# Sink-window attention into a balanced mixture of experts: a new plan of the experts' work, and gathered rows transposed in halves of 64

## The chip, the cores and the metric

One core of one Trainium2 chip runs the whole program as one launch. The metric is device time in microseconds (us), from three timed runs of the kernel before: 525.15, 525.58 and 529.23, median 525.58. All times inside the kernel come from one further execution that was profiled; it took 527.85 us, of which 526.1 us are the span from the first instruction to the last.

## The reference

Attention with 4 batches, 8 heads, 768 positions and head size 64, in which a position sees the first 4 keys and its own 128 last ones; then its rows (3072 x 512) go through a mixture of 8 experts in which every expert gets exactly 384 rows, handed out greedily from the largest logit down:

```python
scores = scale * np.matmul(q, k.transpose(0, 1, 3, 2))
keep = is_sink | in_window
...
a = a / (np.sum(a, axis=-1, keepdims=True) + 1e-09)
x = np.matmul(a, v)            # rows: 3072 x 512
...
logits = x @ w_gate            # 3072 x 8
for idx in np.argsort(-logits.flatten()):
    tok, e = idx // E, idx % E
    if assigned[tok] >= 0 or counts[e] >= 384: continue
    assigned[tok] = e; counts[e] += 1
...
out[mask] = np.maximum(x[mask] @ w1[e], 0.0) @ w2[e]   # 512 -> 1024 -> 512, per expert
```

## The kernel before, in words

The first 155 us of the span are the attention, in 24 blocks of 128 rows. It writes its rows to DRAM (`x_dram`). The change does not touch it. It does hold one thing that matters here: its transposes at L101 and L113 work on 64 rows at a time, the upper and the lower 64 rows of the array side by side, and write to two banks of PSUM.

Then come the experts, one after the other in an order that the router finds out. Router `k` (class `R`, method `phase`) finds the expert that fills up next and its 384 rows. It is a chain of six steps. In each, VectorE compares (`cmp`, L488), TensorE counts (L558, "cnt", 12 or 6 small products), VectorE turns the counts into a decision (`i`, L580), TensorE spreads it (L584, "dp", one small product), and VectorE prepares the next compare. After the sixth step come the ranks (L605, "pp") and the lookup of the row numbers (L631, "ip", 12 small products), from which VectorE writes `idx`.

With `idx`, GpSimd gathers the 384 rows from `x_dram` by three indirect DMAs (L674, G) into `xg0` to `xg2`, 128 rows each. TensorE transposes them (L682, X): 4 column chunks of 128 times 3 row tiles make 12 transposes of 128x128 for each expert, into `pt0` and `pt1`, one PSUM bank for a chunk (for expert 0 also `py0` and `py1`). ScalarE writes the rounded high part `xh` of each chunk (L684), VectorE the remainder `xl` (L685).

SyncE loads an expert's weights in 8 pieces (L665) through 4 buffers `raw`. ScalarE makes the high part `wh` (L667), VectorE the low part `wl` (L669). The first layer (M, L695) has 8x4 steps of three products (`M k.f.c`, for 128 columns `f` of the hidden layer and chunk `c`); its result is split into `hh` on ScalarE (L698) and `hl` on VectorE (L699). The second layer (N, L707) has 3x8 steps `N k.t.f` of three products; ScalarE copies its result to `yo` (L710), and GpSimd scatters it to the output (L712, S). Scatters wait for the one before them to land, and gathers and scatters share GpSimd's queue.

All eight experts, with their routers, are one graph of some 1,800 work pieces (`Graph.add`): an engine, a length in ns, what a piece reads and writes. `ML` holds a delay for each pair of engines (E TensorE, A ScalarE, V VectorE, P GpSimd, S SyncE, D the DMA queue). `Graph.order` is a list planner: it steps through planned time, and on each engine takes, among the pieces that can start within a window (`WIN`) of the earliest, the one of the highest priority: its longest path to the end plus a number for its class (`BIAS`). The order that comes out is the order in each engine's queue. An engine never leaves it: an instruction that waits holds up all behind it. Where the plan shows TensorE idle before the first expert's products, `run` puts filler products there (L534).

Of the kernel before, what the change touches and what calls it, by code (L numbers as in the profile page):

```python
# [377 lines left out]
CAP=384  # L378

STEPS=[(26,64),(20,64),(15,32),(10,32),(5,32),(0,32)]  # L380
ML={'VV':127,'EV':200,'EA':220,'VE':215,'AE':205,'AV':142,'VA':130,'AP':180,'PV':180,'PE':215,'VP':180,'PA':180,'PP':60,'AA':35,'EE':0,
    'VS':900,'SD':1100,'VD':1250,'PD':1250,'AD':1250,'ED':1250,'DA':900,'DV':900,'DP':900,'DE':1070,'DD':0,'EP':220,'PQ':1560,}

class Graph:
# [18 lines left out]
    def order(self,bias,win,free):  # L403
# [37 lines left out]
class Moe:  # L441
# [80 lines left out]
    def pools(self,ctx,w1,w2,x_dram,out):  # L522
# [7 lines left out]
        self.pt=ring(2,[128,512],F32,"pt",ps); self.ph=ring(2,[128,512],F32,"ph",ps); self.py=ring(2,[128,512],F32,"py",ps); self.pr=ring(2,[128,512],F32,"pr",ps)  # L530
# [140 lines left out]
    def rows(self,g,k):  # L671
        nc=self.nc; idx=self.idx[k]; b=k%2
        for t in range(3):
            g.add('P',1038,lambda t=t: nc.gpsimd.indirect_dma_start(out=self.xg[t],out_offset=None,in_=self.x_dram,in_offset=bass.IndirectOffsetOnAxis(ap=idx[:,t:t+1],axis=0)),  # L674
                  [f'idx{k}'],[f'xgi{t}',f'xg{t}'],f'G{k}.{t}',f'G{k}')
            g.add('D',728,None,[f'xgi{t}'],[f'xg{t}'],f'g{k}.{t}',f'G{k}',lat=2300)
        for c in range(4):

            tp,tn=(self.py[c%2],f'py{c%2}') if k==0 and c>1 else (self.pt[c%2],f'pt{c%2}')
            pts=[tn,tn+'.1',tn+'.2']  # L680
            for t in range(3):
                g.add('E',110,lambda t=t,c=c,tp=tp: nc.tensor.transpose(tp[:,128*t:128*t+128],self.xg[t][:,128*c:128*c+128],self.idn),  # L682
                      [f'xg{t}'],[pts[t]],f'X{k}.{c}.{t}',f'X{k}')
            g.add('A',371,lambda c=c,tp=tp: nc.scalar.activation(self.xh[b][:,c,:],tp[:,0:CAP],AF.Copy),pts,[f'xh{b}.{c}'],f'xh{k}.{c}',f'X{k}')  # L684
            g.add('V',469,lambda c=c,tp=tp: nc.vector.tensor_tensor(self.xl[b][:,c,:],tp[:,0:CAP],self.xh[b][:,c,:].bitcast(F32),OP.subtract),pts+[f'xh{b}.{c}'],[f'xl{b}.{c}'],f'xl{k}.{c}',f'X{k}')  # L685

    def mlp(self,g,k):
        nc=self.nc; b=k%2; cls=f'M{k}'; idx=self.idx[k]
        for f in range(8):
            s=(8*k+f//2)%self.NW; p=self.ph[f%2]; pn=f'ph{f%2}'  # L690
            wh,wl=[a[s].rearrange("p (d f) -> p d f",d=4)[:,:,128*(f%2):128*(f%2)+128] for a in (self.wh,self.wl)]
            for c in range(4):
                def mm(c=c,p=p,wh=wh,wl=wl):
                    for i,(x,y) in enumerate(((wh,self.xh[b]),(wh,self.xl[b]),(wl,self.xh[b]))):
                        nc.tensor.matmul(p[:,0:CAP],x[:,c,:],y[:,c,:],start=c==0 and i==0,stop=c==3 and i==2)  # L695
# [141 lines left out]
```

## Time and profile before

| | us |
|---|---|
| median of three runs (525.15 to 529.23) | 525.58 |
| profiled execution | 527.85 |
| its span | 526.1 |
| attention, to the first router product | 155.5 |
| router 0, up to the first row transposes | 155.5 to 184.8 |
| eight experts on TensorE | 184.8 to 519.4 |
| last copy and scatter | to 526.1 |

Busy shares of the span are 91% for TensorE, 72% for VectorE, 44% for ScalarE and 29% for GpSimd. In the experts TensorE is the engine to watch: an idle time of another engine costs nothing unless TensorE waits for it.

### The profile page before, as it was taken

The numbers are of one execution on the slowest core, as the hardware profiler recorded it, in microseconds if no ns is written. First come the engines' busy times: TensorE is split into PE (matmuls) and PEld (weight loads), VectorE is DVE, ScalarE is ACT, GpSimd is POOL, SyncE is SP. The second block draws the span as 40 slices with busy tenths as digits, with TensorE's granted clock in tenths as the row PEclk, the third lists the DMA queues.
The fourth block names the chain that finished last, engine by engine and source line by source line (L and its number), as shares of the span: only waits on it lengthen the run. The fifth ranks groups of instructions, "written<-read, shape, count | busy, mean of one in ns | idle before, by whom it ended". The sixth has DMA issues, their size and how long they took to land. (4 is left out here: it accounts for less than half of the span.)

```text
span 526.1 us, 11023 instructions
## 1 busy us (share of the span) xinstructions
PE 480.9 (91%) x3958; PEld 398.8 (76%) x3958; DVE 378.4 (72%) x1188; ACT 232.4 (44%) x666; POOL 150.3 (29%) x195
## 2 busy tenths in 40 slices
PE   5999999999974779989998998999999989999994
PEld 3788786877862359868877976878878868999983
DVE  3999999999986776876796896897788765542100
ACT  4877887777710342243154262263054254441110
POOL 3886775574410200040033030031041031200011
PEclk8999999999995597997999999999999999999998
DMA  7757666754320640380093272290183395610011
GB/s 224 251 144 208 178 179 171 210 172 127 98 61 1 210 172 1 128 292 20 10 317 116 63 256 83 88 330 25 60 260 121 119 281 199 206 56 21 21 39 41
DMA packets 75319, 73.11 MB, mean 139 GB/s; under 512 B 28544, under 2 KB 57856, under 8 KB 75264
## 3 DMA queue, kind: packets, MB, share of 16 engines
q1 hardware_dynamic: 71424, 59.81, 37.4%
q0 software_dynamic: 3840, 12.59, 6.8%
q8 instruction: 31, 0.51, 0.4%
q14 instruction: 24, 0.20, 0.1%
HBM read 59.80 MB, written 12.58 MB: 138 GB/s over the span
## 5 line engine op out<-in xcount | busy, mean ns | idle before, releaser
L667 ACT ACTIVATE wh<-raw 128x1024 fp32r<-128x1024 f32 x64 | 67.8, 1060 | 102.0 <-DMA raw<-w 61.8
L669 DVE TENSOR_TENSOR wl<-raw,wh 128x1024 fp32r<-128x1024 f32 x64 | 77.9, 1220 | 34.9 <-ACT wh L667 31.7
L695 PE MATMUL ph<-xh,wh 128*128 128x384 f32 x256 | 93.6, 366 | 2.4 <-DVE hl L699 2.4
L695 PE MATMUL ph<-xh,wl 128*128 128x384 f32 x256 | 87.8, 343 | 0.0
L695 PE MATMUL ph<-xl,wh 128*128 128x384 f32 x256 | 87.8, 343 | 0.0
L707 PE MATMUL py<-wh,hh 128*128 128x512 f32 x192 | 78.8, 411 | 0.2 <-ACT yo L710 0.2
L712 POOL DMA_INDIRECT out<-yo,idx x24 | 27.9, 1164 | 177.9 <-ACT yo L710 119.5
L698 ACT ACTIVATE hh<-ph 128x384 fp32r<-128x384 f32 x64 | 30.9, 488 | 107.1 <-PE ph L695 77.4
L707 PE MATMUL py<-wh,hl 128*128 128x512 f32 x192 | 75.7, 394 | 0.1
L707 PE MATMUL py<-wl,hh 128*128 128x512 f32 x192 | 75.6, 394 | 0.0
L95 ACT ACTIVATE P<-pp,nmx 128x132 f32<-128x132 f32 x192 | 68.6, 371 | 8.6 <-DVE nmx L90 8.1
L674 POOL DMA_INDIRECT xg<-x_dram,idx x24 | 29.3, 1221 | 136.1 <-PE py L707 70.5
L80 PE MATMUL pp<-kk,q 64*128 64x260 f32 (+1 forms) x384 | 58.5, 405 | 7.3 <-POOL q L73 3.8
L699 DVE SCALAR_TENSOR_TENSOR hl<-ph,hh 128x384 fp32r<-128x384 f32 x64 | 35.2, 554 | 36.0 <-ACT hh L698 35.4
L695 PEld LDWEIGHTS ph<-xh,wh 128*128 128x128 f32 x256 | 50.2, 196 | 6.6 <-DVE hl L699 4.2
L695 PEld LDWEIGHTS ph<-xl,wh 128*128 128x128 f32 x256 | 49.7, 194 | 1.9
L695 PEld LDWEIGHTS ph<-xh,wl 128*128 128x128 f32 x256 | 49.4, 193 | 0.0
L80 PEld LDWEIGHTS pp<-kk,q 64*128 64x128 f32 x384 | 32.2, 198 | 18.3 <-ACT P L95 7.3
L707 PEld LDWEIGHTS py<-wh,hl 128*128 128x128 f32 x192 | 36.1, 188 | 8.5 <-DVE hl L699 0.5
L707 PEld LDWEIGHTS py<-wh,hh 128*128 128x128 f32 x192 | 36.7, 191 | 6.9 <-issue 1.7
L707 PEld LDWEIGHTS py<-wl,hh 128*128 128x128 f32 x192 | 36.2, 189 | 4.3
L95 ACT ACTIVATION_READ_ACCUMULATOR P<-pp,nmx 128x1 f32 x192 | 39.4, 205 | 0.0
(149 smaller groups left out, 848.3 us busy)
## 6 DMA issues: line engine op xcount, KB each, us to landing
raw<-w SPq DMA_DIRECT2D x64, 512.0 KB, 4.4
v<-vd SPq DMA_DIRECT2D x24, 256.0 KB, 3.2
x_dram<-xt SPq DMA_DIRECT2D x24, 256.0 KB, 2.8
kk<-kd SPq DMA_DIRECT2D x23, 264.0 KB, 5.6
q<-qd SPq DMA_DIRECT2D x23, 256.0 KB, 3.7
us<-ud SPq DMA_DIRECT2D x1, 530.5 KB, 6.1
xg<-x_dram,idx POOLq DMA_INDIRECT x24, 6.3
out<-yo,idx POOLq DMA_INDIRECT x24, 3.2
```

The lines of the kernel that those rows point to most:

```text
L80: PE.matmul(sp[:,s,:n],q[p,g,:],kk[p,g,k0:k0+n],start=True,stop=True)
L95: A.activation(T('P',c)[:,4*s+g,:],sp[:,s,o:o+132],AF.Exp,bias=T('nmx',c)[:,h:h+1],scale=1.0,accum_out=T('sm',c)[:,h:h+1])
L667: g.add('A',947,lambda wh=wh,raw=raw: nc.scalar.activation(wh,raw,AF.Copy),[f'raw{n%4}'],[f'wh{s}'],f'H{k}.{j}',f'W{k}')
L669: g.add(e,{'V':1135,'P':2303}[e],lambda wh=wh,wl=wl,raw=raw,e=e: (nc.vector if e=='V' else nc.gpsimd).tensor_tensor(wl,raw,wh.bitcast(F32) ...
L674: g.add('P',1038,lambda t=t: nc.gpsimd.indirect_dma_start(out=self.xg[t],out_offset=None,in_=self.x_dram,in_offset=bass.IndirectOffsetOnAx ...
L695: nc.tensor.matmul(p[:,0:CAP],x[:,c,:],y[:,c,:],start=c==0 and i==0,stop=c==3 and i==2)
L698: g.add('A',371,lambda f=f,p=p: nc.scalar.activation(self.hh[:,f,:],p[:,0:CAP],AF.Relu),ps,[f'hh{f}'],f'hh{k}.{f}',f'H{k}')
L699: g.add('V',469,lambda f=f,p=p: nc.vector.scalar_tensor_tensor(self.hl[:,f,:],p[:,0:CAP],0.0,self.hh[:,f,:].bitcast(F32),op0=OP.max,op1=OP ...
L707: nc.tensor.matmul(p,x[:,f,ts],w,start=f==0 and i==0,stop=f==7 and i==2)
L712: st=nc.gpsimd.indirect_dma_start(out=self.out,out_offset=bass.IndirectOffsetOnAxis(ap=idx[:,t:t+1],axis=0),in_=y,in_offset=None)
```

## The change

First, the planner gets other numbers: delays (`ML`), lengths of pieces on SyncE, GpSimd and TensorE, the window and the class numbers. A planned gather, for instance, had 1038 ns on GpSimd, 1250 ns to the DMA queue, 728 ns there and 2300 ns after it; now it has 1450, 450, 728 and 150. Transposes now count as small products, after which a large one is planned 90 ns longer.

Second, the transposes. `pt` becomes one pair of PSUM banks. Each gathered tile is transposed in halves: the upper 64 rows go to the first bank, the lower 64 to the second, 64 columns each. For experts 1 to 7 one piece covers all three row tiles and two column chunks (12 half transposes), so there are two such pieces for each expert, the second of which uses the same banks as the first and waits until both chunks are copied out. For expert 0 there is a piece for each tile, and the second half of the columns goes to `py0` and `py1`, from which each chunk is copied out in two instructions instead of one.

```diff
@@ -378,8 +378,8 @@
-ML={'VV':127,'EV':200,'EA':220,'VE':215,'AE':205,'AV':142,'VA':130,'AP':180,'PV':180,'PE':215,'VP':180,'PA':180,'PP':60,'AA':35,'EE':0,
-    'VS':900,'SD':1100,'VD':1250,'PD':1250,'AD':1250,'ED':1250,'DA':900,'DV':900,'DP':900,'DE':1070,'DD':0,'EP':220,'PQ':1560,}
+ML={'VV':127,'EV':207,'EA':225,'VE':140,'AE':170,'AV':153,'VA':140,'AP':395,'VP':860,'PV':200,'PE':215,'PA':200,'PP':60,'AA':35,'EE':0,
+    'VS':150,'SD':2050,'VD':2200,'PD':450,'AD':2200,'ED':2200,'DA':40,'DV':40,'DP':900,'DE':150,'DD':0,'DS':60,'EP':395,'PQ':1560,}
...
-                k=T[i][5][0]!='R'
+                k=T[i][5][0] not in 'RX'
...
-        self.pt=ring(2,[128,512],F32,"pt",ps); self.ph=ring(2,[128,512],F32,"ph",ps); self.py=ring(2,[128,512],F32,"py",ps); self.pr=ring(2,[128,512],F32,"pr",ps)
+        self.tp=ps.tile([128,2,512],F32,name="pt"); self.pt=[self.tp[:,j] for j in (0,1)]; self.ph=ring(2,[128,512],F32,"ph",ps); self.py=ring(2,[128,512],F32,"py",ps); self.pr=ring(2,[128,512],F32,"pr",ps)
...
-        g.add('S',100,load,[f'ei{k}'],[f'reg{k}'],f'reg{k}',f'L{k}')
+        g.add('S',1400,load,[f'ei{k}'],[f'reg{k}'],f'reg{k}',f'L{k}')
...
-                g.add('S',100,lambda: nc.sync.value_load(self.xg[2][0:1,0:1].bitcast(I32)),['xg2'],['rowed'],'rowed','L0')
+                g.add('S',450,lambda: nc.sync.value_load(self.xg[2][0:1,0:1].bitcast(I32)),['xg2'],['rowed'],'rowed','L0')
...
-            g.add('P',1038,lambda t=t: nc.gpsimd.indirect_dma_start(out=self.xg[t],out_offset=None,in_=self.x_dram,in_offset=bass.IndirectOffsetOnAxis(ap=idx[:,t:t+1],axis=0)),
+            g.add('P',1450,lambda t=t: nc.gpsimd.indirect_dma_start(out=self.xg[t],out_offset=None,in_=self.x_dram,in_offset=bass.IndirectOffsetOnAxis(ap=idx[:,t:t+1],axis=0)),
...
-            g.add('D',728,None,[f'xgi{t}'],[f'xg{t}'],f'g{k}.{t}',f'G{k}',lat=2300)
-        for c in range(4):
-
-            tp,tn=(self.py[c%2],f'py{c%2}') if k==0 and c>1 else (self.pt[c%2],f'pt{c%2}')
-            pts=[tn,tn+'.1',tn+'.2']
-            for t in range(3):
-                g.add('E',110,lambda t=t,c=c,tp=tp: nc.tensor.transpose(tp[:,128*t:128*t+128],self.xg[t][:,128*c:128*c+128],self.idn),
-                      [f'xg{t}'],[pts[t]],f'X{k}.{c}.{t}',f'X{k}')
-            g.add('A',371,lambda c=c,tp=tp: nc.scalar.activation(self.xh[b][:,c,:],tp[:,0:CAP],AF.Copy),pts,[f'xh{b}.{c}'],f'xh{k}.{c}',f'X{k}')
-            g.add('V',469,lambda c=c,tp=tp: nc.vector.tensor_tensor(self.xl[b][:,c,:],tp[:,0:CAP],self.xh[b][:,c,:].bitcast(F32),OP.subtract),pts+[f'xh{b}.{c}'],[f'xl{b}.{c}'],f'xl{k}.{c}',f'X{k}')
+            g.add('D',728,None,[f'xgi{t}'],[f'xg{t}'],f'g{k}.{t}',f'G{k}')
+        for d in range(2):
+
+            tp,tn=(self.py,'py') if k==0 and d else (self.pt,'pt')
+            ts=[f'{tn}{i}{x}' for i in (0,1) for x in ('','.1','.2')]
+            def turn(t,d=d,tp=tp):
+                for c in (0,1):
+                    for s in range(2):
+                        p=slice(64*s,64*s+64)
+                        nc.tensor.transpose(tp[s][:,192*c+64*t:192*c+64*t+64],self.xg[t][p,256*d+128*c:256*d+128*c+128],self.idn[p,64*s:64*s+64])
+            if k==0:
+                for t in range(3): g.add('E',125,lambda t=t,turn=turn: turn(t),[f'xg{t}'],ts[t::3],f'X{k}.{d}.{t}',f'X{k}')
+            else: g.add('E',350,lambda turn=turn: [turn(t) for t in range(3)],['xg0','xg1','xg2'],ts,f'X{k}.{d}',f'X{k}')
+            for c in (2*d,2*d+1):
+                o=[x[b][:,c,:].rearrange("p (t s n)->p t s n",s=2,n=64) for x in (self.xh,self.xl)]; l=192*(c-2*d)
+                if tn=='pt': q=[(o,self.tp[:,:,l:l+192].rearrange("p s (t n)->p t s n",t=3))]
+                else: q=[([y[:,:,s] for y in o],tp[s][:,l:l+192].rearrange("p (t n)->p t n",t=3)) for s in (0,1)]
+                for j,((oh,ol),x) in enumerate(q):
+                    g.add('A',371 if len(q)==1 else 209,lambda oh=oh,x=x: nc.scalar.activation(oh,x,AF.Copy),ts,[f'xh{b}.{c}'+'.'*j],f'xh{k}.{c}',f'X{k}')
+                for j,((oh,ol),x) in enumerate(q):
+                    g.add('V',469 if len(q)==1 else 269,lambda oh=oh,ol=ol,x=x: nc.vector.tensor_tensor(ol,x,oh.bitcast(F32),OP.subtract),ts+[f'xh{b}.{c}'+'.'*j],[f'xl{b}.{c}'+'.'*j],f'xl{k}.{c}',f'X{k}')
...
-                g.add('E',522,mm,[f'wh{s}',f'wl{s}',f'xh{b}.{c}',f'xl{b}.{c}']+([pn if c==1 else pn+f'.{c-1}'] if c else []),[pn] if c==0 else [pn+f'.{c}'],f'M{k}.{f}.{c}',cls)
+                g.add('E',528,mm,[f'wh{s}',f'wl{s}',f'xh{b}.{c}',f'xl{b}.{c}']+([f'xh{b}.{c}.',f'xl{b}.{c}.'] if k==0 and c>1 else [])+([pn if c==1 else pn+f'.{c-1}'] if c else []),[pn] if c==0 else [pn+f'.{c}'],f'M{k}.{f}.{c}',cls)
...
-                g.add('E',690,mm,[f'wh{s}',f'wl{s}',f'hh{f}',f'hl{f}']+([pn if f==1 else pn+f'.{f-1}'] if f else []),[pn] if f==0 else [pn+f'.{f}'],f'N{k}.{t}.{f}',cls)
+                g.add('E',695,mm,[f'wh{s}',f'wl{s}',f'hh{f}',f'hl{f}']+([pn if f==1 else pn+f'.{f-1}'] if f else []),[pn] if f==0 else [pn+f'.{f}'],f'N{k}.{t}.{f}',cls)
...
-            g.add('P',1038,put,[f'yo{n%3}',f'idx{k}','outw'],[f'ys{n}'],f'S{k}.{t}',f'Y{k}')
-            g.add('D',728,None,[f'ys{n}',f'yo{n%3}'],['outw'],f's{k}.{t}',f'Y{k}',lat=650)
+            g.add('P',1300,put,[f'yo{n%3}',f'idx{k}','outw'],[f'ys{n}'],f'S{k}.{t}',f'Y{k}')
+            g.add('D',728,None,[f'ys{n}',f'yo{n%3}'],['outw'],f's{k}.{t}',f'Y{k}')
...
-WIN=[57, 20025, 0]
-BIAS={'G0': 295629, 'G1': 162254, 'G2': -279312,
...
+WIN=[95, 25736, 128]
+BIAS={'G0': 1757677, 'G1': 4967512, 'G2': 906277,
...
```

Third, and as a result, the order on every engine differs from 155.5 us on. Three places follow, in rows that name line, operation, output and inputs (the number behind a name tells buffers apart).

GpSimd's queue, from the second gather of expert 1 (`idx_144`) to the first of expert 3 (`idx_146`), before and now:

```order
 L674 DMA xg_2408<-x_dram,idx_144 128x512
-L712 DMA out<-yo_2416,idx_143 3072x512
 L674 DMA xg_2409<-x_dram,idx_144 128x512
-L712 DMA out<-yo_2417,idx_143 3072x512
-L712 DMA out<-yo_2418,idx_143 3072x512
-L712 DMA out<-yo_2416,idx_144 3072x512
+L723 DMA out<-yo_2416,idx_143 3072x512
+L723 DMA out<-yo_2417,idx_143 3072x512
 L674 DMA xg_2407<-x_dram,idx_145 128x512
 L674 DMA xg_2408<-x_dram,idx_145 128x512
 L674 DMA xg_2409<-x_dram,idx_145 128x512
```

The three gathers of expert 1 are now together, and two scatters fewer stand ahead of those of expert 2 (`idx_145`).

ScalarE's queue at the first products of expert 0, before and then now (`wh` 2387 to 2390 are weight pieces 4 to 7, `hh` is the split of the first layer's result):

```order
L667 ACTIVATE wh_2387<-raw_2379 128x1024
L667 ACTIVATE wh_2388<-raw_2380 128x1024
L667 ACTIVATE wh_2389<-raw_2381 128x1024
L698 ACTIVATE hh_2414<-ph_2421 128x384
L667 ACTIVATE wh_2390<-raw_2382 128x1024
L698 ACTIVATE hh_2414<-ph_2422 128x384
```

```order
L667 ACTIVATE wh_2387<-raw_2379 128x1024
L667 ACTIVATE wh_2388<-raw_2380 128x1024
L709 ACTIVATE hh_2414<-ph_2420 128x384
L709 ACTIVATE hh_2414<-ph_2421 128x384
L667 ACTIVATE wh_2389<-raw_2381 128x1024
L709 ACTIVATE hh_2414<-ph_2420 128x384
```

The first two splits have moved ahead of the third of these weight pieces.

TensorE's queue at the first transposes of expert 1, before and then now:

```order
L682 MATMUL pt_2419<-idt,xg_2407 128x128
L682 MATMUL pt_2420<-idt,xg_2407 128x128
L707 MATMUL py_2424<-wh_2389,hh_2414 128x512
L707 MATMUL py_2424<-wl_2401,hh_2414 128x512
L707 MATMUL py_2424<-wh_2389,hl_2415 128x512
```

```order
L558 MATMUL pr_2424<-oh,cmp_109 128x16
L685 MATMUL pt<-idt,xg_2407 128x64 x4
L685 MATMUL pt<-idt,xg_2408 128x64 x4
L685 MATMUL pt<-idt,xg_2409 128x64 x4
L718 MATMUL py_2422<-wh_2387,hh_2414 128x512
```

Before, each gathered tile had its own place in the queue, with products between them; now the first transpose needs all three tiles soon after one another. From the first lookup product of an expert (L631) to the first transpose of its third tile the queue holds, counted in first-layer steps (M), second-layer steps (N) and counts of the next router:

| expert | before | now |
|---|---|---|
| 1 | 15 N, 1 count | 4 M, 8 N, 1 count |
| 2 | 16 N, 2 counts | 8 M, 5 N, 1 count |
| 3 | 3 M, 14 N, 2 counts | 12 M, 6 N, 4 counts |
| 4 | 8 M, 9 N, 1 count | 6 M, 4 N, 2 counts |
| 5 | 5 M, 10 N, 2 counts | 2 M, 9 N, 2 counts |
| 6 | 5 M, 12 N | 3 M, 20 N |
| 7 | 13 M, 3 N | 26 M, 24 N |

On VectorE, between the indices of experts 0 to 5 and the second decision of the router that follows, stand 7, 8, 4, 5, 7 and 1 low parts of weights (L669) before, and 2, 4, 4, 2, 3 and 2 now.

## Rows read from the trace of the kernel before

**Rows 1.** Waits of TensorE from 184.8 us (first row transposes) to 520 us: who waited for whom, us in total, times, longest us.
```profile
PE pt L682 <- DMA xg<-x_dram,idx: 6.0, 6, 2.3
PE pr L584 <- DVE i L580: 3.3, 5, 1.2
PE ph L695 <- DVE hl L699: 2.4, 1, 2.4
PE pr L558 <- DVE cmp L488: 2.1, 4, 1.3
PE pt L682 <- DVE xl L685: 0.8, 1, 0.8
```

**Rows 2.** TensorE in order of time (start us, us, engine, line, operation, xcount, and in brackets the idle time before it and who ended it): the ends of its longest waits in the experts.
```profile
194.90 0.17 PE L584 MATMUL pr<-i,wt 128*128 128x8 bf16 x1 [1.15 <-DVE i L580]
197.45 0.69 PE L695 MATMUL ph<-xh,wh 128*128 128x384 f32 x1 [2.38 <-DVE hl L699]
...
235.36 0.44 PE L682 MATMUL pt<-idt,xg 128*128 128x128 f32 x2 [2.28 <-DMA xg<-x_dram,idx]
```

**Rows 3.** Busy time in two short stretches of the experts: the stretch in us from the span's start, its length, busy us of PE, PEld, DVE, ACT and POOL (instruction counts in brackets), then TensorE's granted clock as a share of full speed, the DMA share and GB/s.
```profile
195.70:202.50 6.80, 5.05 (x16) 5.05 (x17) 4.39 (x10) 2.92 (x5) 0.00 (x0) 0.50 0.01 2
...
236.70:243.50 6.80, 6.03 (x22) 5.15 (x21) 5.56 (x13) 3.09 (x6) 0.99 (x1) 0.50 0.10 39
```

**Rows 4.** TensorE in order of time: a pair of the experts' full transposes (L682) and what follows it; then, from the attention, transposes in halves of 64 rows (L101, L113) with their neighbours.
```profile
185.83 0.38 PE L682 MATMUL py<-idt,xg 128*128 128x128 f32 x2
186.05 0.33 PE L534 MATMUL ph<-grid,onesb 128*128 128x384 bf16 x1
...
100.77 0.41 PE L101 MATMUL pp<-idt,P 64*128 64x64 f32 x8
101.11 0.44 PE L121 MATMUL pp<-A,v 128*64 128x128 f32 x4
101.38 0.39 PE L121 MATMUL pp<-B,v 128*64 128x128 f32 x4
101.59 0.39 PE L121 MATMUL pp<-A,v 128*64 128x128 f32 x4
...
102.69 0.39 PE L121 MATMUL pp<-B,v 128*64 128x128 f32 x4
103.00 0.28 PE L113 MATMUL pp<-idt,ss 64*128 64x64 f32 x2
...
104.05 0.41 PE L101 MATMUL pp<-idt,P 64*128 64x64 f32 x8
104.27 0.38 PE L136 MATMUL pp<-vx,pS 64*128 64x288 f32 x2
```

**Rows 5.** GpSimd's queue in order of time: first and third gather of expert 0, of expert 1 and of expert 2, and the third of expert 7.
```profile
178.31 1.17 POOL L674 DMA_INDIRECT xg<-x_dram,idx  x1 [28.18 <-DVE fin L645]
...
181.47 1.17 POOL L674 DMA_INDIRECT xg<-x_dram,idx  x1 [0.31 <-issue]
222.97 1.34 POOL L674 DMA_INDIRECT xg<-x_dram,idx  x1 [40.33 <-PE py L707]
...
227.68 1.01 POOL L674 DMA_INDIRECT xg<-x_dram,idx  x1 [0.30 <-PE pr L558]
...
273.44 1.54 POOL L674 DMA_INDIRECT xg<-x_dram,idx  x1 [2.79 <-issue]
...
277.08 0.95 POOL L674 DMA_INDIRECT xg<-x_dram,idx  x1 [0.30 <-issue]
...
460.76 0.95 POOL L674 DMA_INDIRECT xg<-x_dram,idx  x1 [0.30 <-PE ph L695]
```

**Rows 6.** TensorE in order of time: the products that look up the indices of expert 1 (L631), the first transposes of the first gathered tile of expert 2, and those of the third tile of expert 7.
```profile
220.28 0.90 PE L631 MATMUL pr<-R,cmp 128*128 128x12 f16 x12
...
278.69 0.44 PE L682 MATMUL pt<-idt,xg 128*128 128x128 f32 x2 [0.50 <-DMA xg<-x_dram,idx]
...
464.77 0.38 PE L682 MATMUL pt<-idt,xg 128*128 128x128 f32 x2
```

**Rows 7.** TensorE in order of time, at full clock: the first product of two successive first-layer steps (L695) and of two successive second-layer steps (L707).
```profile
206.16 0.33 PE L695 MATMUL ph<-xh,wh 128*128 128x384 f32 x1
...
206.68 0.33 PE L695 MATMUL ph<-xh,wh 128*128 128x384 f32 x1
...
222.50 0.39 PE L707 MATMUL py<-wh,hh 128*128 128x512 f32 x1
...
223.19 0.39 PE L707 MATMUL py<-wh,hh 128*128 128x512 f32 x1
```

**Rows 8.** TensorE in order of time: one step of router 0, beside which VectorE does nothing else (L558 counts, L584 decides).
```profile
162.60 0.46 PE L558 MATMUL pr<-oh,cmp 128*128 128x32 bf16 x6 [0.41 <-DVE cmp L488]
163.91 0.17 PE L584 MATMUL pr<-i,wt 128*128 128x8 bf16 x1 [0.85 <-DVE i L580]
...
165.15 0.46 PE L558 MATMUL pr<-oh,cmp 128*128 128x32 bf16 x6 [0.73 <-DVE cmp L488]
```

**Rows 9.** VectorE's group for the low parts of the weights (count, busy us, mean ns of one, idle before it and its releasers).
```profile
L669 DVE TENSOR_TENSOR wl<-raw,wh 128x1024 fp32r<-128x1024 f32 x64 | 77.9, 1220 | 34.9 <-ACT wh L667 31.7 <-PE ph L695 2.6 <-issue 0.3
```

**Rows 10.** ScalarE in order of time, just before the second of these waits ends.
```profile
195.38 1.06 ACT L667 ACTIVATE wh<-raw 128x1024 fp32r<-128x1024 f32 x1 [1.97 <-DMA raw<-w]
196.34 0.47 ACT L698 ACTIVATE hh<-ph 128x384 fp32r<-128x384 f32 x1
```

More of the change, by code (lines that the diff above doesn't have):

```diff
@@ L740 @@
 WARM=[2, 2, 2, 1, 1, 1, 3]
-WIN=[57, 20025, 0]
-BIAS={'G0': 295629, 'G1': 162254, 'G2': -279312, 'G3': 1563873, 'G4': 1916835, 'G5': 932476, 'G6': 733051, 'G7': -243162, 'H0': -37865, 'H1': 19849, 'H2': 91381, 'H3': 988353, 'H4': 747095, 'H5': 376035, 'H6': -482536, 'H7': 1000667, 'L0': 868944, 'L1': 361431, 'L2': -470007, 'L3': -1363030, 'L4': 41186, 'L5': 77034, 'L6': 79739, 'L7': -945789, 'M0': -1013394, 'M1': -1229497, 'M2': -103038, 'M3': 69487, 'M4': 187558, 'M5': 618607, 'M6': -184857, 'M7': -185071, 'R0': 20465, 'R1': 1980837, 'R2': 72703, 'R3': 62626, 'R4': 606374, 'R5': 360221, 'R6': 645534, 'R7': -18418, 'T0': 265289, 'T1': -260247, 'T2': 771717, 'T3': -353978, 'T4': 507303, 'T5': 923769, 'T6': 1091256, 'W0': -324369, 'W1': -204177, 'W2': 520839, 'W3': 15091, 'W4': 717057, 'W5': 73461, 'W6': 506221, 'W7': 639832, 'X0': 584716, 'X1': 216444, 'X2': 327140, 'X3': 730156, 'X4': 747134, 'X5': 763428, 'X6': 1245410, 'X7': 235969, 'Y0': 1049838, 'Y1': -1062891, 'Y2': -751289, 'Y3': -323402, 'Y4': -991979, 'Y5': -1207049, 'Y6': -429487, 'Y7': -379383}
+WIN=[95, 25736, 128]
+BIAS={'G0': 1757677, 'G1': 4967512, 'G2': 906277, 'G3': 4965447, 'G4': 2497292, 'G5': 3709954, 'G6': 4999776, 'G7': 11345473, 'H0': 3618737, 'H1': 11234355, 'H2': 3293123, 'H3': 4969292, 'H4': 9964481, 'H5': 3833237, 'H6': 9470979, 'H7': -339849, 'L0': 3791508, 'L1': 1088135, 'L2': 11356101, 'L3': 5112529, 'L4': 5428807, 'L5': 1756123, 'L6': 1097952, 'L7': 1473479, 'M0': -2542971, 'M1': 1827967, 'M2': 2135185, 'M3': 3832861, 'M4': 1815393, 'M5': 1169409, 'M6': -2404742, 'M7': -2412157, 'R0': 3296436, 'R1': 5978167, 'R2': 12660829, 'R3': 5375989, 'R4': 11417141, 'R5': 7929148, 'R6': 5465804, 'R7': 1759715, 'T0': 9472168, 'T1': 2206185, 'T2': 3740408, 'T3': 3282440, 'T4': 11433655, 'T5': 5481308, 'T6': 12213190, 'W0': 2243130, 'W1': -1759397, 'W2': -1985466, 'W3': 881245, 'W4': 3482193, 'W5': 2305330, 'W6': -3015399, 'W7': 7830404, 'X0': 2372639, 'X1': 824705, 'X2': 10920704, 'X3': 2134624, 'X4': 8053908, 'X5': 3841811, 'X6': 1525393, 'X7': 923312, 'Y0': 3171892, 'Y1': 3397961, 'Y2': 1136554, 'Y3': 1416609, 'Y4': 3283572, 'Y5': 976324, 'Y6': 953287, 'Y7': 1229408}
 def attention_general(ctx,tc,qd,kd,vd,iwd,ident,idn,x_dram,L,n_sink,window):
```

## The prediction

> **What bounds the kernel now.** I read the waits of TensorE first, then its work in order of time, the granted clock by stretch, and the queues of GpSimd, ScalarE and VectorE around the waits. From the first row transposes on, TensorE is all but full, and what it loses there is a short list: waits of 6.0 us for gathered rows, 3.3 and 2.1 us for the router's chain on VectorE (decisions and compares), 2.4 us for a split of the first layer, 0.8 us for a remainder of the rows [rows 1]. The reader should see that these are few and long: 2.38 us after 1.15 us near 195 us, and 2.28 us at 235 us [rows 2]. Around both, the granted clock stands at 0.50, the lower of the two levels (1.2 GHz), for 6.8 us. TensorE was busy for 5.05 and 6.03 us of these, and work at half clock takes twice as long, so half of it, 2.5 and 3.0 us, is lost [rows 3]. So 14.6 us of waits and 5.5 us of clock are what a new plan can win, beside the work itself.
>
> **Transposes.** Before, two full transposes take 0.22 us [rows 4], so an expert's 12 take 1.32 and all 96 take 10.6 us. In the attention eight halves take 0.22 us from the start of L101 to the next operation in the same 64-row form [rows 4]. An expert has 24 halves now, 0.66 us, all 192 take 5.3 us: 5.3 us saved. Against it stands the change of form. Entering 64-row work after 128-row work took 0.31 us from L121 to L113, where successive L121 groups take 0.21: 0.10 more. Leaving it took 0.34 instead of 0.22 us, and the next group 0.27 instead of 0.21: 0.18 more [rows 4]. There are 16 such visits now, two for each expert. At 0.28 us they cost 4.5 us. Their neighbours in the attention are not the experts' products, but no nearer row exists; the bounds are 0 and 4.5 us, and I take 4.5. The transposes give -0.8 us (-5.3 to 0). The Trainium skill (TensorEngine Tiling, Tiling Modes) says that a change of the tiling mode drains TensorE, which speaks against this change, and that rows of 64 allow up to twice the speed; the rows above agree with both.
>
> Copying out costs no more: the same ScalarE and VectorE instructions for experts 1 to 7, and for expert 0 two more on each, beside filler products. The second piece of an expert waits until the first is copied out, about 1.5 us (estimate: two splits of 0.47 us one after the other [rows 10] and a remainder of about that length). The shortest distance between two such pieces in the new queue is two second-layer steps and a count, 2 x 0.69 + 0.9 = 2.3 us, so nothing waits.
>
> **Waits for gathered rows.** From the first lookup product of expert 1 to its first gather were 222.97 - 220.28 = 2.7 us [rows 5, 6]; from first to third gather 3.2 us at expert 0 and 3.6 at expert 2; and from the start of a gather to the transpose that waited for it 5.25 us at expert 2 and 7.7 at expert 1, where weights were loading beside it, while expert 7, with quiet queues, needed no more than 4.0 [rows 2, 5, 6]. So the third tile is there 2.7 + 3.2 + 5.25 = 11.1 us after the lookup begins (9.9 to 14.0). I take 5.25 because that transpose did wait, with weights under way as they mostly are. Now count what the new queue has to do meanwhile: the lookup itself 0.9 us [rows 6], a first-layer step 0.52, a second-layer step 0.69 [rows 7], a count of 12 products about the same 0.9, of six 0.46 [rows 8]. The table of the section on the change gives 9.4 us for expert 1, 9.4 for 2, 14.0 for 3, 8.6 for 4, 10.0 for 5, 16 and more for 6 and 7. So transposes wait 1.7, 1.7, 2.5 and 1.1 us at experts 1, 2, 4 and 5: 7.0 us where 6.0 were, +1.0 us (with the bounds, 2.3 to 18.6 us in all: -3.7 to +12.6). This is the point of the change I trust least: the new plan allows 1450 + 450 + 728 + 150 ns = 2.8 us for a gather that takes 5.
>
> **Waits for the router.** They were 5.4 us [rows 1]. With nothing else on VectorE, a step needs 1.31 us from count to decision and 1.24 from decision to count [rows 8]. What stretches it is foreign work in VectorE's queue, above all low parts of weights, 1.22 us each, which themselves stand idle 31.7 us for ScalarE [rows 9]. Before, 32 of these stood between an expert's indices and the second decision of the next router, now 17. Products that cover a step got fewer in the new queue (about 0.3 us fewer in each of 66 gaps: from 1.6 to 1.3 us, and from 2.0 to 1.7, by the lengths of rows 6 to 8), but still cover the undisturbed chain. I take 1.0 us of waits left: -4.4 us (-5.4 to the price of the last rival).
>
> **The split, the remainder, the start.** The 2.38 us wait came from ScalarE: the split `hh` stood behind the weight piece that arrived at 195.38 [rows 10]. It is now ahead of it in the queue. The remainder's 0.8 us goes with the order of the chunks. Together -3.2 us (-3.2 to 0). What is late next is the router. At expert 0 the second count now stands before the first product, and its 1.24 us [rows 8] are covered by fillers only: +1.2 us (0 to +2).
>
> **Clock.** Waits of about 2 us come at three places in place of two. I take one fall of the clock instead of two, since none is as long as the pair at 195 us: -2.7 us (-5.5 to +2.8).
>
> **Sum.** -0.8 + 1.0 - 4.4 - 3.2 + 1.2 - 2.7 = -8.9 us against the profiled execution's own 527.85 us, 519.0. The profiled execution is 2.3 us above the median of the runs, 525.58. The same change from the median gives 516.7 us, which is what I forecast. The attention and the first router keep their order and the tail its steps, so they count nothing.
>
> **Rivals.** *Gathers land as the plan thinks.* Quiet queues gave 4.0 us, and the new plan puts the gathers of expert 1 together and fewer scatters ahead of them. Then only 2.3 us of gather waits remain (-4.7 more), and the clock does not fall (-2.8 more): 516.7 - 7.5 = 509.2 us. The Trainium skill (DMA: Bandwidth & Descriptors, Anatomy of one DMA, GpSimd path) puts such a transfer at 2.0 us plus its bytes over 436 GB/s, 2.6 us for 256 KB by its figures as an estimate; the trace shows 4.0 to 7.7, and the measurement decides.
>
> *Waits take the place of waits.* The gathers land as late as expert 1's did, with all three tiles needed at once: 18.6 us at the ceiling, 11.6 more than I took. Half of that, 5.8, is plausible, and one more fall of the clock costs 2.8: 516.7 + 8.6 = 525.3 us, no change.
>
> *The halves don't overlap.* If upper and lower half ran one after the other, 192 halves would take 10.6 us, nothing saved: 516.7 + 5.3 = 522 us, no change. Against it: they do overlap at L101 with the same instruction [rows 4].
>
> *The router becomes the bound, and the kernel slower.* Its gaps are covered 0.3 us less. If VectorE's foreign work fills the chain so that this becomes wait in each of 66 gaps, it costs 20 us on TensorE, 516.7 + 20 = 537. It makes the kernel slower by 1% from 0.21 us a gap on (516.7 + 14 = 530.8). Against it: on average the old waits are 5.4 / 66 = 0.08 us a gap, and few gaps make them.
>
> **Numbers.** Chances: the forecast, 511 to 520.3, 0.48; gathers as planned 0.22; waits for waits 0.16; no overlap 0.05; router 0.09. One per cent of 525.58 is 5.3 us, about what a measurement here can tell from no change. The first two cases are faster: 0.70. The next two are the same: 0.21. The last is slower: 0.09. A range from 508 to 526 holds the forecast, most of the first rival and most of the two cases of no change, some 8 in 10, and reaches from gathers and clock at their good ends to the late gathers.
>
> **What would show it.** The transposes' group should have 192 entries in pairs a few ns apart, 0.33 us for a piece of 12. TensorE's waits should name the gathers first, 1 to 2.5 us at experts 1, 2, 4 and 5, with under 1.5 us for decisions and compares together, and none of a microsecond for `hl`. One stretch at 0.50 clock should stand after such a wait, beside that of router 0. The last product should end near 511 us. I am wrong if waits for `i` and `cmp` add up to more than 5 us, if gather waits pass 12, or if three stretches have the lower clock.

## The result, and the profile after

The changed kernel takes 512.81 us (median of four runs, 510.85 to 514.88) where the kernel before took 526.19 beside it: a ratio of 0.974 (95% interval 0.968 to 0.979). Its profiled execution took 512.72 us, 15.1 us less than that of before. The forecast was 516.7, in a range from 508 to 526. Here and below a median counts every timed execution, while a ratio leaves out those more than 1.5% above the fastest of the same kernel.

The waits of TensorE in the changed kernel from 184.7 to 515 us (who waited for whom, us in total, times, longest us) answer to [rows 1]:

```profile
PE pt L685 <- DMA xg<-x_dram,idx: 1.7, 2, 1.5
PE ph L706 <- DVE hl L710: 1.3, 3, 0.6
PE pr L584 <- DVE i L580: 0.7, 2, 0.4
PE pr L558 <- DVE cmp L488: 0.6, 2, 0.4
```

Of 14.6 us, 4.3 are left. Both waits for rows are at expert 0. The longer one (1.53 us) ends at the first transpose, so it lies ahead of the stretch that [rows 1] cover: with their 14.6 compare 2.8 us. A transpose of experts 1 to 7 waits for nothing. TensorE in order of time at the first transposes of expert 0, at a piece of expert 1 and at the last product (start us, us, operation, count, in brackets the idle time before it and who ended it), for [rows 2, 4]:

```profile
184.80 0.34 PE L685 MATMUL pt<-idt,xg 64*128 64x64 f32 x4 [1.53 <-DMA xg<-x_dram,idx]
...
221.12 0.59 PE L685 MATMUL pt<-idt,xg 64*128 64x64 f32 x12
221.64 0.50 PE L718 MATMUL py<-wh,hh 128*128 128x512 f32 x1
...
503.79 0.39 PE L718 MATMUL py<-wh,hl 128*128 128x512 f32 x1
```

The last product ends at 504.2 us in place of 519.4; the first transpose starts where it did (184.8). So the experts' stage, from the first transpose to the end of the last product, went from 334.6 to 319.4 us, and holds the whole gain. After the first rows the clock fell once, for 3.4 us, beside filler products. The stretch (length, busy us of PE, PEld, DVE, ACT, POOL, granted clock, DMA share, GB/s) answers to [rows 3]:

```profile
185.90:189.40 3.50, 3.50 (x21) 1.77 (x19) 2.21 (x7) 1.76 (x6) 0.00 (x0) 0.51 0.41 136
```

### The profile page after: what moved, and what is told of

The parts are those of the page before. It is cut to its first block, busy times and chain, and to the rows that moved or that the text cites. A ratio compares the mean times of both kernels' runs of the same rounds, so it can differ in the third digit from the quotient of the medians.

```text
span 511.0 us, 11188 instructions
## 1 busy us (share of the span) xinstructions
PE 475.7 (93%) x4058; PEld 394.0 (77%) x4058; DVE 387.4 (76%) x1190; ACT 232.6 (46%) x668; POOL 146.3 (29%) x195
## 4 chain that ended last, share of the span: by engine, by line
PE 57%; DVE 32%; issue 3%; ACT 3%; DMA 3%; SPq 1%; POOL 1%; POOLq 0%; DVEq 0%; ACTq 0%
PE ph L706 17%; PE py L718 16%; PE pp L80 7%; PE pp L121 7%; DVE wl L669 6%; DVE cmp L488 4%; PE pp L139 3%; DVE hl L710 2%; PE pp L101 2%; DVE xl L696 2%; PE pr L558 2%; ACT P L95 1%; DMA xg<-x_dram,idx 1%; DVE nmx L90 1%; DVE odd L579 1%
## 5 line engine op out<-in xcount | busy, mean ns | idle before, releaser
L706 PE MATMUL ph<-xh,wh 128*128 128x384 f32 x256 | 91.2, 356 | 1.4 <-DVE hl L710 1.3
L669 DVE TENSOR_TENSOR wl<-raw,wh 128x1024 fp32r<-128x1024 f32 x64 | 77.9, 1217 | 18.0 <-ACT wh L667 17.8
L706 PE MATMUL ph<-xh,wl 128*128 128x384 f32 x256 | 86.4, 338 | 0.0
L706 PE MATMUL ph<-xl,wh 128*128 128x384 f32 x256 | 86.3, 337 | 0.0
L723 POOL DMA_INDIRECT out<-yo,idx x24 | 26.5, 1105 | 181.5 <-ACT yo L721 124.8
L674 POOL DMA_INDIRECT xg<-x_dram,idx x24 | 26.5, 1106 | 122.1 <-issue 53.3
L706 PEld LDWEIGHTS ph<-xh,wh 128*128 128x128 f32 x256 | 48.7, 190 | 5.1 <-DVE hl L710 2.3
L706 PEld LDWEIGHTS ph<-xl,wh 128*128 128x128 f32 x256 | 48.3, 189 | 1.7
L706 PEld LDWEIGHTS ph<-xh,wl 128*128 128x128 f32 x256 | 48.1, 188 | 0.0
```

The source lines that it names most:

```text
L669: g.add(e,{'V':1135,'P':2303}[e],lambda wh=wh,wl=wl,raw=raw,e=e: (nc.vector if e=='V' else nc.gpsimd).tensor_tensor(wl,raw,wh.bitcast(F32) ...
L674: g.add('P',1450,lambda t=t: nc.gpsimd.indirect_dma_start(out=self.xg[t],out_offset=None,in_=self.x_dram,in_offset=bass.IndirectOffsetOnAx ...
L723: st=nc.gpsimd.indirect_dma_start(out=self.out,out_offset=bass.IndirectOffsetOnAxis(ap=idx[:,t:t+1],axis=0),in_=y,in_offset=None)
```

## Experiments

The stage is the measure for single profiles, since the attention ahead of it, the same in all kernels, took from 154.9 to 158.5 us to the first router product. Per profile: its length, TensorE's waits behind the first transpose, the time at 1.2 GHz in it (the granted clock's record), and what is left after taking off the waits and half of that time (an estimate of what half clock loses; it counts idle time too, so it is a little high, and what is left a little low where much of the stage ran at half clock). "Ratio" is that of the times to the kernel before.

| kernel | ratio (95%) | stage | waits | at half clock | left |
|---|---|---|---|---|---|
| before | 1 | 334.6 | 14.8 | 13.6 | 313.0 |
| changed, two profiles | 0.974, 0.973 (0.964 to 0.983) | 319.4, 317.9 | 2.8, 2.8 | 3.4, 0 | 314.9, 315.1 |
| changed, full transposes | 0.976 (0.971 to 0.981) | 318.2 | 2.6 | 0 | 315.6 |
| changed, old delays | 0.979 (0.971 to 0.988) | 320.3 | 5.0 | 0 | 315.3 |
| new numbers on old transposes | 0.998 (0.994 to 1.002) | 333.1 | 10.5 | 13.6 | 315.8 |
| old numbers, halves alone | 1.012 (1.006 to 1.018) | 340.2 | 16.9 | 17.1 | 314.7 |
| before, one split first | 0.996 (0.992 to 1.001) | 332.9 | 14.2 | 6.8 | 315.3 |
| changed, loads at 1, 2, 4, 5 | 1.022 (1.013 to 1.032) | 343.3 | 19.3 | 23.9 | 312.1 |
| changed, loads at 3, 6, 7 | 0.991 (0.987 to 0.996) | 325.3 | 6.1 | 6.8 | 315.8 |
| changed, fills on GpSimd | 0.995 (0.990 to 1.000) | 327.9 | 9.2 | 6.8 | 315.3 |
| changed, reads on GpSimd | 0.993 (0.989 to 0.996) | 322.9 | 6.0 | 3.4 | 315.1 |

The last column is the reading to take along: whatever the order and either form of transpose, TensorE's work is 312 to 316 us. Stages differ by 25 us, and almost all of it is waits and the clock behind them.

**Full transposes in the new order.**

```diff
-for c in (0,1):
-    for s in range(2):
-        p=slice(64*s,64*s+64)
-        nc.tensor.transpose(tp[s][:,192*c+64*t:192*c+64*t+64],self.xg[t][p,256*d+128*c:256*d+128*c+128],self.idn[p,64*s:64*s+64])
+for c in (0,1): nc.tensor.transpose(tp[c][:,128*t:128*t+128],self.xg[t][:,256*d+128*c:256*d+128*c+128],self.idn)
```

> The changed kernel with its order of work kept, but the rows turned by full 128x128 transposes, six to a piece, as before. My theory: twelve halves cost what six full ones cost, because the saved 0.33 us of a piece goes into the change of form, so the time stays within 1.5 us of the changed kernel's 512.8 (I expect 513.6), and a piece with the operation behind it takes about as long in both traces. Rival one: the change of form costs nothing, the halves save the full 5.3 us, and this kernel comes near 518. Rival two: the change of form costs more than it saves, and this kernel is faster, near 510.

Measured: 512.72 us, ratio 0.976, the changed kernel's within the intervals. TensorE at one piece between two first-layer products (the second piece of expert 4), with full transposes and then in the changed kernel:

```profile
330.56 0.34 PE L701 MATMUL ph<-xh,wl 128*128 128x384 f32 x1
330.74 0.82 PE L682 MATMUL pt<-idt,xg 128*128 128x128 f32 x6
331.31 0.42 PE L701 MATMUL ph<-xh,wh 128*128 128x384 f32 x1
331.57 0.34 PE L701 MATMUL ph<-xl,wh 128*128 128x384 f32 x1
```

```profile
329.25 0.34 PE L706 MATMUL ph<-xh,wl 128*128 128x384 f32 x1
329.52 0.59 PE L685 MATMUL pt<-idt,xg 64*128 64x64 f32 x12
330.04 0.44 PE L706 MATMUL ph<-xh,wh 128*128 128x384 f32 x1
330.31 0.34 PE L706 MATMUL ph<-xl,wh 128*128 128x384 f32 x1
```

The twelve halves hold the next product off for 0.52 us, the six full ones for 0.57. But the halves themselves start 0.27 us after the product ahead of them, the full ones 0.18. From that product to the second one behind the piece it is 1.06 us with halves and 1.01 with full transposes; summed over the 14 pieces of experts 1 to 7, 16.8 and 16.6. Over the stage 318.2 stands against 317.9 in the changed kernel's second profile, neither of which waits over 0.2 us for a row; the two profiles of the changed kernel differ by more. My theory holds: the halves gain nothing, and 5.3 us are excluded. This kernel is as good as the changed one, not better.

**Halves alone; new numbers alone.** The first is the changed code planned with the old `ML`, lengths, `WIN` and `BIAS`; the second is the old transposing code with the new ones.

```diff
-WIN=[95, 25736, 128]
+WIN=[57, 20025, 0]
...
```

> The halves and their PSUM pair alone: the change's new code for the transposes, ordered by the planner with the old lengths, delays, window and classes' values. My theory: the halves by themselves are worth less than 1 us, and what the change wins comes from the order; so this is within 4 us of the kernel before, 522 to 530, with waits of TensorE of the old kind (gathers, decisions, compares, a split) of 10 us or more. Rival: the halves and the fewer, larger pieces carry the gain, and it is below 517 with less than 7 us of such waits.

> The new numbers alone: the planner's new lengths, delays, window and classes' values on the old code for the transposes (three full ones for each chunk, each chunk copied out by itself, the old two banks). My theory: the numbers carry most of the gain, so it lies near the changed kernel, 513 to 519, and gathers land sooner than before (median under 5 us in place of 6.3). Rival one: the values were found for one set of steps and are worth nothing on another; then it is like the kernel before or slower, 524 to 535. Rival two: the halves carry the gain, same time.

Measured: 531.91 and 525.14 us. Neither half of the change carries the gain; the first is slower than before, and above the 522 to 530 that I had expected. The waits of the new numbers on the old transposes:

```profile
PE pt L682 <- DMA xg<-x_dram,idx: 4.4, 6, 1.5
PE pr L584 <- DVE i L580: 2.5, 5, 0.9
PE ph L695 <- DVE hl L699: 1.6, 5, 0.7
PE pr L558 <- DVE oh L509: 1.2, 1, 1.2
PE pr L558 <- DVE cmp L488: 0.8, 3, 0.4
```

I had expected 513 to 519 there; rival one holds. Its gathers landed in 4.5 us in the median. (The 6.3 in the expectation is the median of the 3 landings, of 24, that the trace of before tells; in the same order with one pair exchanged, below, it is 5.0 over all 24.) Yet rows were still waited for six times: the planner had other pieces of work to place.

**Old class values; old delays.** Two runs on the changed code split the numbers; the second also plans large products behind transposes as before, without the 90 ns.

```diff
-BIAS={'G0': 1757677, ...
+BIAS={'G0': 295629, ...
```

```diff
-    'VS':150,'SD':2050,...
+    'VS':900,'SD':1100,...
```

> The changed kernel with the window and the classes' values of before; the new lengths and delays and the halves stay. After the two runs in which halves alone and numbers alone brought nothing: my theory is that the values were found for one set of steps, lengths and delays, and hold for that set only; so this lies at 520 to 533, with 8 us or more of waits. Rival: truer lengths and delays give a better plan with any values; then under 517.

> The changed kernel with the planner's lengths and delays of before; the window, the classes' values and the halves stay. My theory, as for the run with the old values: 518 to 533, since the old delays let a gather count 1.1 us less from its start than the new ones or put the steps in another place, and the waits for rows come back. Rival: the values carry the order and the delays hardly move it; then under 516.

Measured: 536.81 us with the old window and class values (ratio 1.016, 1.004 to 1.029), worse even than expected, and 515.7 with the old lengths and delays. My theory fell for the second: gather waits did not come back (0.2 us in all), and the stage is 0.9 and 2.4 us over the changed kernel's two. So the window and class values on the new pieces of work carry the order, and the new lengths and delays add little.

**One pair exchanged in the kernel before.** `hh0.0` goes ahead of the weight piece `H0.6` on ScalarE [rows 10].

```diff
+x=ev.pop(at('H0.6')); ev.insert(at('hh0.0')+1,x)
```

> The kernel before with one pair on ScalarE exchanged: the split hh of the first layer's first group goes ahead of the weight piece that it stood behind. My theory: the wait of 2.38 us near 195 us goes, and with it the stretch of half clock from 195.7 to 202.6 that lost 2.5 us; so 4 to 5 us faster than before, about 521.5. Rival one: the wait goes, but the clock falls all the same after the 1.15 us that stand ahead of it: 2.4 us faster, 523.8. Rival two: the order behind it was fitted to the wait, the late weight piece or the router's chain stops TensorE next, and the time stays within 1 us of before.

Measured: 525.03 us, ratio 0.996 (0.992 to 1.001). The wait of 2.38 us did shrink to 0.30, and the clock no longer fell there. Its waits over the stage:

```profile
PE pt L682 <- DMA xg<-x_dram,idx: 5.4, 8, 1.3
PE pr L584 <- DVE i L580: 4.6, 6, 2.2
PE pr L558 <- DVE cmp L488: 2.6, 3, 1.7
PE ph L695 <- DVE hl L699: 1.4, 2, 1.1
```

At the first product this order is 0.2 us ahead, at 243 us of before 7.1; by the end 2.6 are left (516.84 against 519.41). Between lie a wait of 1.72 us for `cmp` at 315 us and two new stretches of half clock, at 316.0 and 387.7 us. What rival two said would happen did, over the whole run: the sum of waits hardly moves (14.2 after 14.8), the work runs into the next late result. Whether the gain stays within its 1 us is open: the median is 2.0 us under before, and the interval reaches from no gain to 4 us.

**Gathers crowded.** Four loads of weights that nothing reads, put into SyncE's queue behind the first gather of an expert and released by its indices.

```diff
+nc=self.nc; nc.sync.value_load(self.idx[k][0:1,0:1],min_val=0,max_val=B*S)
+for d in range(4): nc.sync.dma_start(self.dump[d].rearrange("p (d f) -> p d f",d=4),self.w1[0:1,:,256*d:256*d+256].rearrange("o (d p) f -> p (o d) f",p=128))
```

> The changed kernel with four more loads of 512 KB from the weights beside the gathers of experts 1, 2, 4 and 5, each group released by the same indices as the gathers; nothing reads what they bring. My theory: a gather lands late because other transfers share the queues' engines with it; so landings at these four experts rise from 3.3 to 5 us (after's values) to 5 to 8, TensorE waits 1 to 3 us for rows at each of them, 4 to 12 us in all, and the time is 5 to 14 us above 512.8. Rival one: landing depends on GpSimd's issue alone; the landings stay under 5 us at these experts and the time within 1 us. Rival two: the extra loads delay the weights behind them on SyncE's queue, and TensorE waits for low parts of weights, not for rows.

> The same four extra loads, but beside the gathers of experts 3, 6 and 7, where the changed order has 15, 16 and over 30 us from lookup to transpose. My theory: landings of these gathers rise in the same way (5 to 9 us), yet no transpose waits for them, so the time stays within 2 us of 512.8; what costs is not the late landing but the short cover. Rival: the extra traffic itself costs (weights late, half clock), and the time rises as in the kernel with the loads at experts 1, 2, 4 and 5.

Measured: 538.09 and 520.74 us. From issue to landing the gathers took, in the changed kernel and then with loads at experts 1, 2, 4 and 5:

```profile
DMA to landing us min/median/max: 3.3/3.8/7.6
```

```profile
DMA to landing us min/median/max: 3.3/6.1/7.6
```

and TensorE's waits with these loads were:

```profile
PE pr L584 <- DVE i L580: 8.3, 3, 7.6
PE pt L685 <- DMA xg<-x_dram,idx: 6.2, 7, 1.7
PE py L718 <- ACT yo L721: 3.7, 1, 3.7
```

So traffic beside a gather makes it late, and where the cover (the work between lookup and first transpose) is about 10 us, TensorE waits: 1.70 and 1.37 us in one piece of expert 4, 5.1 at experts 1, 4 and 5 (the rest of the 6.2 is at expert 0). But the kernel is 25 us slower, where I had expected 5 to 14, and the larger part comes as rival two began, with late weights, though TensorE then waits for the decision and a copied result behind them, not for low parts. ScalarE shows it, where the wait of 7.6 us begins:

```profile
271.46 1.06 ACT L667 ACTIVATE wh<-raw 128x1024 fp32r<-128x1024 f32 x1 [9.25 <-DMA raw<-w]
272.42 0.47 ACT L709 ACTIVATE hh<-ph 128x384 fp32r<-128x384 f32 x1
```

The weights queued behind the loads come late, ScalarE stands 9.25 us for one piece, and `hh`, `hl` and the decision queue up behind it. At experts 3, 6 and 7 the three gathers of expert 3 took 7.5 us in the median (4.1 in the changed kernel), and no transpose waited, as expected: cover decides. The time still rose by 8 us, where I had expected under 2, by the same way (2.7 us for an `hh` behind a weight piece for which ScalarE stood 6.0 us) and by a stretch of half clock of 3.4 us behind it; a second such stretch is at expert 0, where the changed kernel's first profile has one too.

**Gathers delayed, without traffic.** Two ways of holding GpSimd for a while between the first gather and the second, at experts 1, 2, 4 and 5.

```diff
+for d in range(2): self.nc.gpsimd.memset(self.dump[d],0.0)
```

```diff
+for d in range(3): self.nc.gpsimd.value_load(self.idx[k][0:1,0:1],min_val=0,max_val=B*S)
```

> The changed kernel with the second and third gathers of experts 1, 2, 4 and 5 issued about 2 us later, behind two fills of a tile that nothing reads on GpSimd; no transfer is added. From after's trace the third tile is there 8.6, 9.1, 9.2 and 8.9 us after the lookup begins, and the piece of transposes starts at 9.8, 10.5, 9.3 and 10.6 us. My theory, that what counts is the cover of each gather against its need and nothing else: waits of about 0.8, 0.7, 1.9 and 0.3 us, 3.7 in all, rows landing as soon after their issue as in the changed kernel, and the experts' stage from the first transpose to the last product longer by that, 3 to 4.5 us, without a further stretch of half clock, since no wait reaches 2 us. Rival one: each wait brings a stretch of half clock, and the stage is 7 us or more longer. Rival two: other waits hide it (the late gathers push scatters and loads apart), and the stage is under 2 us longer.

> The changed kernel as it is, on the same chip, for a second profile: its experts' stage within 1 us of the first one's 319.4 us, its landings within 0.3 us of the first ones in the median, and no wait over 0.6 us after the first expert's rows. If landings or waits differ by more than that, they belong to the execution and not to the order of the work.

> The same delay without fills: behind the first gather of experts 1, 2, 4 and 5 GpSimd reads three words of that expert's indices into registers, which nothing uses; by such reads on SyncE (0.6 to 0.7 us from a read to its last step) the second and third gathers start about 2 us later. The run before stopped VectorE too: the operation beside the two fills took 2.13 us where it takes 0.22. My theory: without that, what is left is cover against need: waits for rows of 0.8, 0.7, 1.9 and 0.3 us for a delay of 2 us (less by the same amount, if the delay turns out shorter), no operation of VectorE stretched, no wait of 2 us for decisions, compares or splits, and the experts' stage 3 to 5 us longer than the 317.9 us of the changed kernel's second profile. Rival: the stage is again about 10 us longer, with waits of VectorE's results over 2 us; then the late rows themselves throw the order behind them out, and the fills had little to do with it.

Measured: 523.28 us with the fills, 520.31 with the reads, 512.23 unchanged. The unchanged kernel's second profile repeats the first: landings 3.3, 3.7 and 7.2 us (minimum, median, maximum), no wait over 0.6 us, stage 317.9. That is 1.5 us shorter, where I had allowed 1: the clock stretch at expert 0 is gone, as are the 1.53 us ahead of the stage; both belong to the execution.

The fills were a bad instrument. The stage is 327.9 us, 8.5 and 10 longer than the changed kernel's two, as rival one's number has it, but only 1.5 of its 9.2 us of waits are for rows behind the first expert. GpSimd and VectorE beside the fills at expert 2:

```profile
255.29 1.86 POOL L751 MEMSET dump<- 128x1024 f32 x2
```

```profile
255.06 2.13 DVE L646 TENSOR_SCALAR pen<-fin 128x24 f32<-128x24 f32 x1
257.23 0.18 DVE L499 TENSOR_TENSOR vm<-pen,v 128x24 f32<-128x24 f32 x1
```

VectorE's small operation takes 0.22 us in the changed kernel; here it ends with the fills, and the count behind it waits 2.0 us for `cmp`. The Trainium skill (SBUF — State Buffer, Who interferes with whom) says that such an operation, when it uses both of VectorE's port pairs, and a GpSimd instruction exclude each other for the whole of the one that came first. This trace agrees that one holds the other; by its records VectorE's operation begins 0.23 us ahead of the fills, so it does not show that the first one wins. At experts 4 and 5 single-input operations (L507 to L514) were held in the same way, for 0.9 to 2.2 us; at expert 1 an operation with two inputs (L509) and a reduction (L505) ran beside the fills in their usual 0.36 and 0.35 us.

With reads in place of fills the second and third gathers were 0.9 to 1.3 us late, not 2, and no VectorE operation stretched. TensorE and GpSimd at expert 4:

```profile
325.02 0.46 PE L685 MATMUL pt<-idt,xg 64*128 64x64 f32 x8
327.73 0.34 PE L685 MATMUL pt<-idt,xg 64*128 64x64 f32 x4 [2.25 <-DMA xg<-x_dram,idx]
```

```profile
318.43 1.08 POOL L674 DMA_INDIRECT xg<-x_dram,idx  x1 [10.98 <-DVE idx L638]
320.73 0.96 POOL L674 DMA_INDIRECT xg<-x_dram,idx  x1 [1.22 <-PE pr L558]
322.00 1.39 POOL L674 DMA_INDIRECT xg<-x_dram,idx  x1 [0.30 <-issue]
```

Issued at 322.00, the third tile was usable at 327.73, 5.7 us later, where in the changed kernel it took 3.8. The reason offered by the trace, not tested alone: SyncE's next weight loads start at 322.6, 0.6 us behind this gather, while in the changed kernel they came 1.5 us behind it; 0.73 MB of weights moved until the tile was used, 0.11 until it landed in the changed kernel. Rows were waited for three times, 3.3 us in all, and after the 2.25 us the clock fell:

```profile
328.60:331.90 3.30, 3.30 (x13) 3.17 (x12) 2.11 (x7) 1.81 (x3) 0.00 (x0) 0.50 0.48 165
```

The stage is 322.9, 5.0 us longer than in the second profile: 3.2 more of waits and 1.7 of clock. The rival (10 us from late rows alone) falls. My theory's 3 to 5 us came, but not by its sum: for gathers 0.9 to 1.3 us late, with landings unchanged, it gives some 0.9 us of waits (its own figures, each less by what is missing from 2 us), and the rest came from a later landing and from the clock, which it did not count. The timed median rose by more than this profile, 8 us; the profiled execution was the fastest of ten.

## Why the prediction was right

The sign, the size (within 4 us of the median, 6 of the profiled execution) and the mechanism (waits and clock, not work) were right. In the stage, waits fell by 12.0 us where the forecast has 6.6 (+1.0 - 4.4 - 3.2), half clock gave back 3.8 where it has 2.7, and the rest grew by 0.6 where it has 0.4 (-0.8 + 1.2): -15.2 for -8.9. Term by term, against the profiled executions:

- **Transposes, -0.8.** Nothing, rather: the 14 pieces take 16.8 us as halves and 16.6 as full transposes. With the 0.33 us a piece that I took as saved, the change of form comes to about 0.35, where I had 0.28. The bounds of this term were added up wrong: 5.3 us saved less 0 to 4.5 is -5.3 to -0.8, not to 0.
- **Waits for rows, +1.0.** The step that failed: "the third tile is there 2.7 + 3.2 + 5.25 = 11.1 us after the lookup begins". These are the rows for expert 4, the shortest cover (lookup and first transposes, then the first and third gather):

```profile
316.75 0.41 PE L631 MATMUL pr<-R,cmp 128*128 128x12 f16 x4
...
326.04 0.59 PE L685 MATMUL pt<-idt,xg 64*128 64x64 f32 x12
```

```profile
319.45 1.08 POOL L674 DMA_INDIRECT xg<-x_dram,idx  x1 [10.97 <-issue]
...
322.13 0.95 POOL L674 DMA_INDIRECT xg<-x_dram,idx  x1 [0.30 <-issue]
```

 Lookup to first gather 2.70 us (2.7 taken), first to third 2.68 (3.2 taken), landing 3.8 (5.25 taken): 9.2 us. The cover was 9.3 (8.6 taken), so this expert had 0.1 us to spare (experts 1, 2 and 5 had 1.3 to 1.7). At these four no wait came where I had put 7.0 us; behind the first transpose 6.0 us became 0.2. I had taken the landing from an order in which gathers ran among weight loads, and carried it into one in which most do not. In the order of before (with one pair exchanged) the median landing is 5.0 us, in the new one 3.8; while the three gathers of expert 4 were under way, 2.5 MB of weights moved there and 0.1 MB here, and the crowded gathers above show what such traffic does. The rival "gathers land as the plan thinks" had what happened; its reason (gathers together, fewer scatters ahead) fits the 2.68 us between the gathers, not the landing. The time fell between the two, 512.8 between 516.7 and 509.2.
- **Waits for the router, -4.4.** Right: 5.4 us became 1.3, -4.1. The rival in which the router becomes the bound did not come near.
- **Split and remainder, -3.2.** Nearly: no wait over 0.6 us for `hl`, but three of these make 1.3 us, so -1.9 with the remainder's 0.8. The exchange of the pair alone shows what the prediction did not weigh: by itself this step is worth 2.0 us of median (the interval reaches to none), because the next late result takes over.
- **Start, +1.2.** Right in the second profile: from the first transpose to the first product it is 4.5 us where it was 3.5, +1.1. In the first profile it is 6.1, +2.7, with half clock and a wait of 0.2 us in it.
- **Clock, -2.7.** Too small a gain, and it goes with the second point: I had put one fall behind a wait for rows at experts 1 to 5, and neither the wait nor the fall came. 5.5 us were lost before; after, the first profile loses at most 1.7 beside fillers at expert 0, the second nothing.

The two failed terms lean the same way, which is why the gain was larger than forecast: waits for rows that did not come, and the clock that would have fallen after them. Of the signs announced, the 192 entries (180 on `pt` and 12 on `py`; the starts of a piece of 12 spread over 0.36 us), the small sums for `i`, `cmp` and `hl` and the absence of a wait of a microsecond for `hl` were there; the gather waits at experts 1, 2, 4 and 5 were not, the stretch of half clock stood in one of two profiles and at expert 0, and the last product ended at 504, not 511.

What stays open: why the new class values fit the new pieces and not the old ones. The runs show that they do (0.974 and 0.998), not whether a search on the old transposes would have found as good an order.

## What to carry to other kernels

Where one engine is all but full in a stage, write the stage as work, waits and the time at the lower clock; if the work column does not move between versions, only the order is left to win. Count the cover of each transfer in steps, but take its need from the traffic that the new order will put beside it, not from the old one: a gather here took 3.3 to 7.6 us. Removing one wait alone can be worth little if the next late result is close behind (2 us of the 4 to 5 expected here), and a plan's fitted numbers can hold for one set of work pieces only: here 0.974 on it and 0.998 on another.

## What the runs showed of the hardware

- An indirect gather of 128 rows landed 3.3 to 4.1 us after its issue where less than 0.3 MB of weights moved meanwhile, and 5.0 to 7.6 where it was 1 MB or more (changed kernel, first profile); adding four loads of 512 KB beside it made 7.5 us out of 4.1 at expert 3.
- Two fills of 128x1024 on GpSimd held a 128x24 operation of VectorE with one input for 2.13 us in place of 0.22; beside such fills, an operation with two inputs and a reduction kept their 0.36 and 0.35 us.
- Twelve 64-row half transposes between first-layer products took 1.06 us from the product ahead to the second one behind, six full transposes 1.01: what the halves save, the change of form takes.
- The length of a single wait did not tell whether the clock falls. The granted clock went to 0.50 during waits of 2.15, 2.31, 2.38, 3.68 and 7.57 us and 0.7 to 1.4 us after the end of waits of 2.0, 2.25, 2.28 and 2.67 us, for 3.4 to 10.2 us; but not after one of 2.26 us (with the fills, at 330 us), nor after 1.49 and 1.54 us (with the old delays). In the kernel with new numbers on old transposes it fell three times behind waits of 0.99, of 0.94 and 0.30, and of 1.25 and 0.90 us. In the changed kernel's second profile, with no wait over 0.6 us, it stayed at full level to the end of the products.
- The attention, the same instructions in every kernel, took between 154.9 and 158.5 us to the first router product from one execution to the next. Differences of 1% in a whole time should be sought in the stage itself.
